# Products with an unread result on TensorE, ahead of q and of each pair's scores, in a block of cached attention

## The chip, the cores and the metric

The kernel runs on one core of a Trainium2 chip. A core has five engines with queues of their own: TensorE (PE; its weight loads are listed as PEld), VectorE (DVE), ScalarE (ACT), GpSimd (POOL) and SyncE (SP), which here only issues transfers. Transfers run on 16 DMA engines. The metric is the time of one execution in device microseconds; the number given for a kernel is the median of its runs.

## The reference

A block of attention with grouped heads over a cache: 8 sequences, 4 new tokens each, 32 query heads, 8 key and value heads, 2048 cached positions, head size 128, everything in bfloat16.

```python
q = (x @ wq).reshape(B, Sq, Hq, Dh).transpose(0, 2, 1, 3)   # x: 8 x 4 x 512, wq: 512 x 4096
k = jnp.repeat(k_cache, 4, axis=1)                          # k_cache, v_cache: 8 x 8 x 2048 x 128
v = jnp.repeat(v_cache, 4, axis=1)
scores = jnp.einsum("bhqd,bhkd->bhqk", q, k) * Dh ** -0.5
o = jnp.einsum("bhqk,bhkd->bhqd", softmax(scores), v)
out = o.transpose(0, 2, 1, 3).reshape(B, Sq, Hq * Dh) @ wo  # wo: 4096 x 512
```

Keys and values are 33.5 MB each, the two weights 4.2 MB each: 75.5 MB are read once.

## The kernel before

The work on the cache goes in eight pairs, one for each sequence `p`, and in sixteen units of values `u`, two for each sequence (four key and value heads each).

**Transfers.** SP issues all loads into one queue, in the order of the program: the keys of pair 0, `x`, `wq`, the keys of pair 1, the values of sequence 0, then for each pair the keys of a later pair (4 MB, `load_pair`, L95) and two units of values (2 MB each, `load_v`, L100), as the buffers come free, and last `wo` in six pieces (`load_wo`, L106, with the list `pieces` at L407). A key buffer is free when VectorE has turned its last tile; a buffer of values when TensorE has used it.

**Start.** TensorE turns `x` by products with an identity (L141, `xtp`), multiplies it with `wq` (`q_products`, L154, 32 products in two groups), and ScalarE, VectorE and GpSimd scale and spread the result over `q_bd` (L168 to L190).

**A pair.** Its keys are turned on VectorE in four tiles `kt` (`turn_keys`, L127; three buffers). Each tile gives eight score products on TensorE (`scores`, L207), 128x512 each, into two PSUM tiles `s_ps`, which ScalarE's exponentials of the pair before must have left. When all four are there, VectorE takes the maxima (L229), ScalarE the exponentials (L248), VectorE turns the probabilities (L262), and ScalarE and GpSimd copy them into a block form (`copy_probs`, L269). The values of a unit are 32 products 128x256 in four quarters (`values`, L312); they run about two pairs behind the scores, as `values_of` (L419) lists. ScalarE divides the result (L332), and `finish` (L342) turns it by one float32 product with 64 columns (`o_t`, L355), which VectorE copies.

**Order.** The order on each engine is that of the program, written by hand. In pair `p`, TensorE has: scores of tiles 0 and 1, two quarters (16 products) of the first unit of values, scores of tile 2, `finish` of the last pair's units, scores of tile 3, then the other quarters of values. In pairs 0, 3 and 4 VectorE turns the next pair's first tile ahead of the maxima (L449).

```python
        scores(p, 0)
        scores(p, 1)
        for quarter in range(2) if vals else ():
            values(vals[0], quarter)
        if (p, 2) not in kts:
            turn_keys(p, 2)
        scores(p, 2)
```

**Tail.** After pair 7, units 11 to 15 of the values run one after the other on TensorE, with `finish` of the unit before within each; then `project` (L396) multiplies with `wo` in the order of its pieces, VectorE and ScalarE copy the result, and SP stores it.

**PSUM.** `xtp`, the two `psq` of q, every `o_t`, and `nat` and `perm` of the tail share two buffers with the tag "m" in the pool `psum_m` (L69): each takes the buffer of the one before the last, and waits until that has been read.

Of the kernel before, what the change touches and what calls it, by code (L numbers as in the profile page):

```python
# [9 lines left out]
FP32 = mybir.dt.float32  # L10
# [4 lines left out]
def kernel(  # L15
# [9 lines left out]
    nc = tc.nc  # L25

    B, Sq, D = x.shape
    _, Hkv, Sk, Dh = k_cache.shape
# [40 lines left out]
    psum_m = ctx.enter_context(tc.tile_pool(name="psum_m", bufs=2, space=bass.MemoryType.PSUM))  # L69
# [8 lines left out]
    ident4 = const.tile([128, 128], FP32, name="ident4")  # L78
# [48 lines left out]
    def turn_keys(p, t):  # L127
        kts[(p, t)] = ktpool.tile([128, CT, 2, 2, SH, 2], BF16, tag="kt", name="kt")
        nc.vector.transpose(  # L129
            kts[(p, t)][:, :, :, :, :, :].rearrange("k c w j s e -> k (c w j s e)").bitcast(FP32),  # L130
            k_sb[p % KB][:, t * CT : (t + 1) * CT, :].rearrange("s c d -> s (c d)").bitcast(FP32),
        )
# [5 lines left out]
    for i in range(XR):  # L138
        row = x_all[:, i * D : (i + 1) * D].rearrange("q (p r) -> q r p", r=R)
        for r in range(R):  # L140
            nc.tensor.matmul(  # L141
                xtp[:, r, i::XR],
                lhsT=row[:, r, :],
                rhs=ident[:T, :T:XR],
                start=True,
                stop=True,
# [4 lines left out]
        v_cache[0].rearrange("(v g) (s c) d -> (g s) v c d", v=VB, c=C),  # L151
    )

    def q_products(j):  # L154
        psq = psum_m.tile([128, rep * Dh], FP32, tag="m", name="psq")
        for r in range(R):
            for g in range(G):
                c0 = (2 * g + j) * rep * Dh
                nc.tensor.matmul(  # L159
                    psq[g * T : (g + 1) * T, :],  # L160
                    lhsT=xT_sb[:, r, :],
                    rhs=wq_sb[:, r, c0 : c0 + rep * Dh],
                    start=(r == 0),
                    stop=(r == R - 1),
                )
        return psq

    def scale_q(psq):  # L168
        q_nat = small.tile([128, rep * 2, 2, S], BF16, tag="q_nat", name="q_nat")
        nc.scalar.mul(  # L170
            out=q_nat[:, :, :, :],
            in_=psq[:, :].rearrange("t (n w e) -> t n e w", w=S, e=2),
            mul=scale,
        )
        return q_nat

    def spread_q(j, q_nat, engines):
        q_t = small.tile([128, rep, 4, B, Sq], BF16, tag="q_t", name="q_t")
        nc.vector.transpose(  # L179
            q_t[:, :, :, :, :].rearrange("w h i b s -> w (h i b s)"),  # L180
            q_nat[:, :, :, :].rearrange("t n e w -> t (n e w)"),
        )
        for g in range(G):
            rows = slice(g * S, (g + 1) * S)
            engines[g](  # L185
                out=q_bd[rows, j, :, :, :, g ^ (2 * j), :].rearrange(
                    "w k e b (h s) -> w (k e b) h s", h=rep
                ),
                in_=q_t[rows, :, :, :, :].rearrange("w h i b s -> w (i b) h s"),
            )  # L190

    by_gpsimd = nc.gpsimd.tensor_copy
    by_three = [by_gpsimd, nc.vector.tensor_copy, nc.scalar.copy] * 3
    q_nats = [scale_q(q_products(j)) for j in range(2)]
    spread_q(0, q_nats[0], by_three)
    spread_q(1, q_nats[1], by_three[1:])
# [10 lines left out]
    def scores(p, t):  # L207
        if t == 0:
            for j in range(2):
                s_pss[(p, j)] = psum_s.tile([128, 2, CT, SH], FP32, tag="s", name="s_ps")  # L210
        for i in range(4):
            k, e = i // 2, i % 2
            for j in range(2):
                h = (t + j) % 2
                nc.tensor.matmul(  # L215
                    s_pss[(p, j)][h * NQ : (h + 1) * NQ, t // 2, :, :],
                    lhsT=q_bd[:, j, k, e, p, :, :].rearrange("k g q -> k (g q)"),
                    rhs=kts[(p, t)][:, :, k, j, :, e],
                    start=(i == 0),
                    stop=(i == 3),  # L220
                )
# [26 lines left out]
    def exponentials(u):  # L248
        s_sbs[u] = small.tile([128, C // 4, S, 2], BF16, tag="s_sb", name="s_sb")
        l_sbs[u] = totals.tile([128, 1], FP32, tag="l_sb", name="l_sb")  # L250
        nc.scalar.activation(  # L251
            out=s_sbs[u][:, :, :, :].rearrange("q a w j -> q a j w"),
            in_=s_pss[u][:, :, :, :].rearrange("q i c s -> q c s i"),
            func=EXP,
            bias=less[u][:, 0:1],
            accum_out=l_sbs[u][:, :],
        )
# [4 lines left out]
    def turn_probs(u):  # L262
        p_ts[u] = turned.tile([128, C // 4, 2, HQ, 2], BF16, tag="p_t", name="p_t")
        nc.vector.transpose(  # L264
            p_ts[u][:, :, :, :, :].rearrange("s x g q j -> s (x g q j)").bitcast(FP32),
            s_sbs[u][:, :, :, :].rearrange("q a s j -> q (a s j)").bitcast(FP32),
        )
# [44 lines left out]
    def values(u, quarter):  # L312
        if quarter == 0:
            o_pss[u] = psum_o.tile([128, 2, Dh], FP32, tag="o", name="o_ps")
        h, a0 = quarter // 2, quarter % 2 * (C // 8)
        for a in range(C // 8):
            c = quarter * C // 4 + 2 * a
            nc.tensor.matmul(  # L318
                o_pss[u][:, :, :].rearrange("n j d -> n (j d)"),
                lhsT=probs_of[u][:, h, a0 + a, :, :, :].rearrange(  # L320
                    "s j g q -> s (j g q)"
                ),
                rhs=vs[u][:, c : c + 2, :].rearrange("s c d -> s (c d)"),
                start=(c == 0),
                stop=(c == C - 2),
            )
# [15 lines left out]
    def finish(u):  # L342
        v, b = units[u]
        o_t = psum_m.tile([128, NQ], FP32, tag="m", name="o_t")
        if u == NU - 1:
            for h in range(2):
                nc.tensor.matmul(
                    o_t[:, :],
                    lhsT=o_scs[u][:, h, :],
                    rhs=ident4[:, h * NQ : (h + 1) * NQ],  # L350
                    start=(h == 0),
                    stop=(h == 1),
                )
        else:
            nc.tensor.matmul(o_t[:, :], lhsT=o_scs[u][:, :], rhs=both[:, :], start=True, stop=True)  # L355
        (nc.scalar.copy if u in (NU - 3, NU - 1) else nc.vector.tensor_copy)(  # L356
            out=oT[v][:, :, :, b, :].rearrange("d (k r) p s -> d p k r s", k=2),
            in_=o_t[:, :].rearrange("d (k p r s) -> d p k r s", k=2, p=2, s=Sq),
        )
# [51 lines left out]
    def all_inverses():  # L411
        while waiting:
            inverses(*waiting.pop(0))

    def softmax_top(u):
        maxima(u)
        exponentials(u)

    values_of = [(), (), (0, 1), (2,)] + [(2 * p - 5, 2 * p - 4) for p in range(4, NPAIR)]  # L419
    after = {w: w + 2 for w in range(NU - 7)}  # L420
    after.update({NU - 6: NU - 4, NU - 5: NU - 3, NU - 4: NU - 2, NU - 3: NU - 1})
# [3 lines left out]
    for p in range(NPAIR):  # L425
        vals = values_of[p]
        for t in range(2):
            if (p, t) not in kts:
                turn_keys(p, t)
        scores(p, 0)  # L430
        scores(p, 1)
        for quarter in range(2) if vals else ():
# [4 lines that stand above are left out]
        turn_keys(p, 3)  # L437
        for w in values_of[p - 1] if p else ():
            finish(w)
        scores(p, 3)  # L440
        if p == NPAIR - 1:
            for u in (NU - 5, NU - 2):
                probs_of[u] = ktpool.tile(
                    [128, 2, C // 4, 2, G, HQ], BF16, tag="kt", name="last_probs"
                )
                words = probs_of[u][:, :, :, :, :, :].rearrange("s x a j g q -> s (x a j g q)")
                nc.gpsimd.memset(words.bitcast(FP32), 0.0)
            copy_probs(NU - 5)
        if p in (0, 3, 4):  # L449
            turn_keys(p + 1, 0)  # L450
        softmax_top((p, 0))
        softmax_top((p, 1))
        for j in range(2):
            turn_probs((p, j))
            if j == 0:
                all_inverses()
        for i, w in enumerate(vals):
            for quarter in range(0 if i else 2, 4):
                values(w, quarter)
            divide(w)  # L460
            if w in after:
                copy_probs(after[w])
            if i == 0:
                waiting += sums(p)
        if p < 2:
            waiting += sums(p)
        if p == 0:
            copy_probs(0)
            copy_probs(1)
        for load in loads_after[p]:  # L470
            (load_pair if load[0] == "p" else load_v)(int(load[1:]))
# [64 lines left out]
```

## Time and profile before

| | |
|---|---|
| time, median of 3 runs | 187.11 us (186.83 to 187.14) |
| profiled execution, its own time | 187.1 us |
| its span, first to last instruction | 185.2 us |
| mean granted TensorE clock over the span | 0.879 |
| TensorE products busy | 124.2 us (67%), 962 instructions |
| TensorE weight loads busy | 80.5 us (43%), 962 instructions |
| VectorE busy | 128.4 us (69%) |
| ScalarE busy | 73.7 us (40%) |
| GpSimd busy | 68.6 us (37%) |
| main DMA queue, share of 16 engines' span | 95.6% |

All times of the profile are from one execution, in us from the start of its span. Busy time of TensorE is modelled from the pipelined products. The clock row gives, for each fortieth of the span, the share of full speed that the throttle granted. A row of a timeline has start, duration, engine, line, operation, written and read tile, shape and count, and in brackets how long the engine was idle before it and which instruction ended that.

### The profile page before, as it was taken

To read this page: it belongs to the slowest core of one execution; us is meant where nothing else is said; L and a number is where in the kernel's file an instruction comes from. 1 tells how busy PE (TensorE), PEld (TensorE's weight loads), DVE (VectorE), ACT (ScalarE), POOL (GpSimd) and SP (SyncE) were. 2 spreads that over 40 slices of the span, in tenths; PEclk is the share of its full clock that TensorE was granted. 3 is DMA by queue.
4 is the path that set the end of the run, shared out by engine and by line. 5 is a ranking of instruction groups with operands and counts; after the bars stand their busy time and mean duration, and the time that the engine had idled before them with its cause. 6 is when DMAs were issued, how large, how long until landed. Compare 5 with 4: busy or idle time off the path is not lost.

```text
span 185.2 us, 2591 instructions
## 1 busy us (share of the span) xinstructions
PE 124.2 (67%) x962; PEld 80.5 (43%) x962; DVE 128.4 (69%) x170; ACT 73.7 (40%) x129; POOL 68.6 (37%) x171
## 2 busy tenths in 40 slices
PE   0002078637505993793499859839985998999993
PEld 0002023212202582362156636715562567988972
DVE  6119335979779788969887798798479857654110
ACT  2000031078060039603900792892089439556030
POOL 8800021028421236322403382470247375872000
PEclk9999999965755899699669999985996599999999
DMA  6999999999999999999989999999999999999950
GB/s 227 453 439 425 432 411 425 428 471 428 403 432 460 446 386 455 412 421 478 446 379 428 442 448 396 432 457 418 435 421 432 432 421 439 428 425 416 420 203 7
DMA packets 4515, 75.71 MB, mean 409 GB/s; under 512 B 500, under 2 KB 660, under 8 KB 916
## 3 DMA queue, kind: packets, MB, share of 16 engines
q1 hardware_dynamic: 4504, 75.57, 95.6%
q8 instruction: 7, 0.11, 0.2%
q14 instruction: 4, 0.03, 0.0%
HBM read 75.53 MB, written 0.03 MB: 408 GB/s over the span
## 4 chain that ended last, share of the span: by engine, by line
PE 49%; DVE 29%; DMA 10%; ACT 5%; issue 5%; SPq 0%; ACTq 0%
PE o_ps L318 28%; DVE kt L129 19%; PE s_ps L215 13%; DMA wq_sb<-in_wq_dram 10%; ACT s_sb L251 4%; DVE top L233 4%; DVE p_t L264 3%; PE out_ps L399 2%; PE psq L159 2%; PE o_t L355 2%; DVE swapped L225 1%; DVE v_both L113 1%; DVE less L239 1%; PE perm L384 1%; PE nat L368 1%
## 5 line engine op out<-in xcount | busy, mean ns | idle before, releaser
L129 DVE STREAM_TRANSPOSE kt<-k_sb 128x2048 f32<-128x2048 f32 x32 | 71.2, 2274 | 10.0 <-DMA k_sb<-in_k_cache_dram 7.9
L215 PE MATMUL s_ps<-kt,q_bd 128*64 128x512 bf16 x256 | 47.3, 492 | 35.6 <-DVE kt L129 23.9
L318 PEld LDWEIGHTS <-probs 128*128 128x128 bf16 x448 | 45.1, 103 | 14.0 <-issue 6.1
L280 POOL COPY probs<-p_t 32x512 bf16<-32x512 bf16 x53 | 32.3, 610 | 43.3 <-PE o_ps L318 41.1
L251 ACT ACTIVATE s_sb<-s_ps,less 128x1024 bf16<-128x1024 f32 x16 | 22.3, 1393 | 64.6 <-DVE less L239 37.3
L215 PEld LDWEIGHTS <-q_bd 128*64 128x64 bf16 x256 | 17.9, 131 | 58.8 <-issue 33.6
L280 ACT COPY probs<-p_t 32x512 bf16<-32x512 bf16 x50 | 30.8, 616 | 1.3 <-DVE p_t L264 0.3
L318 PE MATMUL o_ps<-v_both,probs 128*128 128x256 bf16 x192 | 23.8, 284 | 0.0
L233 DVE TENSOR_REDUCE top<-s_ps 128x1 f32<-128x1024 f32 x16 | 19.4, 1215 | 5.2 <-PE s_ps L215 5.2
L318 PE MATMUL o_ps<-v_more,probs 128*128 128x256 bf16 x160 | 22.1, 302 | 0.0
L225 POOL COPY l_swapped<-l_sb 64x1 f32<-64x1 f32 x32 | 5.8, 180 | 30.5 <-ACT s_sb L251 29.7
L264 DVE STREAM_TRANSPOSE p_t<-s_sb 128x512 f32<-128x512 f32 x16 | 11.3, 709 | 6.8 <-ACT s_sb L251 6.8
L299 POOL TENSOR_TENSOR l_total<-l_sb,l_swapped 32x1 f32<-32x1 f32 x64 | 12.3, 192 | 4.0
L338 ACT ACTIVATE o_sc<-o_ps,r_sb 64x128 f32<-64x128 f32 x28 | 10.1, 359 | 4.7 <-PE o_ps L318 2.8
L356 DVE CAST oT<-o_t 128x64 bf16<-128x64 f32 x14 | 3.1, 225 | 12.0 <-PE o_t L355 12.0
L318 PE MATMUL o_ps<-k_sb,probs 128*128 128x256 bf16 x96 | 11.5, 273 | 0.0
L170 ACT ACTIVATE q_nat<-psq 128x512 bf16<-128x512 f32 x2 | 1.2, 597 | 24.1 <-PE psq L159 24.1
L141 PE MATMUL xtp<-ident,v_both 32*128 32x4 bf16 x32 | 1.2, 169 | 13.8 <-DMA v_both<-in_x_dram 13.8
L159 PE MATMUL psq<-wq_sb,xT_sb 128*32 128x512 bf16 x32 | 3.6, 629 | 8.1 <-DMA wq_sb<-in_wq_dram 8.1
L185 POOL COPY q_bd<-q_t 32x512 bf16<-32x512 bf16 x3 | 2.1, 687 | 18.1 <-DVE q_t L179 18.0
L141 PEld LDWEIGHTS <-v_both 32*128 32x128 bf16 x32 | 1.1, 111 | 13.7 <-issue 13.7
L122 POOL MEMSET probs<- 128x4096 bf16 x2 | 7.0, 3512 | 0.0
(46 smaller groups left out, 85.3 us busy)
## 6 DMA issues: line engine op xcount, KB each, us to landing
k_sb<-in_k_cache_dram SPq DMA_DIRECT2D x8, 4096.0 KB, 19.2
v_more<-in_v_cache_dram SPq DMA_DIRECT2D x6, 2048.0 KB, 22.7
v_both<-in_v_cache_dram SPq DMA_DIRECT2D x4, 2048.0 KB, 21.0
k_sb<-in_v_cache_dram SPq DMA_DIRECT2D x4, 2048.0 KB, 22.1
wq_sb<-in_wq_dram SPq DMA_DIRECT2D x1, 4096.0 KB, 19.3
v_both<-in_v_cache_dram SPq DMA_DIRECT2D x1, 4096.0 KB, 28.0
wo_sb<-in_wo_dram SPq DMA_DIRECT2D x3, 1024.0 KB, 14.9
wo_sb<-in_wo_dram SPq DMA_DIRECT2D x1, 640.0 KB, 16.9
```

The costliest lines, as they stand in the source:

```text
L122: nc.gpsimd.memset(pr[:, :, :, :, :, :], 0.0)
L129: nc.vector.transpose(kts[(p, t)][:, :, :, :, :, :].rearrange("k c w j s e -> k (c w j s e)").bitcast(FP32), k_sb[p % KB][:, t * CT : (t + ...
L159: nc.tensor.matmul(psq[g * T : (g + 1) * T, :], lhsT=xT_sb[:, r, :], rhs=wq_sb[:, r, c0 : c0 + rep * Dh], start=(r == 0), stop=(r == R - 1),)
L215: nc.tensor.matmul(s_pss[(p, j)][h * NQ : (h + 1) * NQ, t // 2, :, :], lhsT=q_bd[:, j, k, e, p, :, :].rearrange("k g q -> k (g q)"), rhs=k ...
L225: engine.tensor_copy(out=out[h * NQ : (h + 1) * NQ, :], in_=in_[(1 - h) * NQ : (2 - h) * NQ, :])
L233: nc.vector.reduce_max(out=top[:, :], in_=s_pss[u][:, :, :, :].rearrange("q i c s -> q (i c s)"), axis=AX,)
L251: nc.scalar.activation(out=s_sbs[u][:, :, :, :].rearrange("q a w j -> q a j w"), in_=s_pss[u][:, :, :, :].rearrange("q i c s -> q c s i"), ...
L264: nc.vector.transpose(p_ts[u][:, :, :, :, :].rearrange("s x g q j -> s (x g q j)").bitcast(FP32), s_sbs[u][:, :, :, :].rearrange("q a s j ...
L280: by[x * G + col](out=probs_of[u][rows, x, :, :, col, :], in_=p_ts[(b, j)][quad * S : (quad + 1) * S, :, col % 2, :, :].rearrange("s x q j ...
L299: nc.gpsimd.tensor_tensor(out=total[rows, :], in0=l_sbs[(p, j)][rows, :], in1=swapped[j][rows, :], op=ADD)
L318: nc.tensor.matmul(o_pss[u][:, :, :].rearrange("n j d -> n (j d)"), lhsT=probs_of[u][:, h, a0 + a, :, :, :].rearrange("s j g q -> s (j g q)"),
L338: nc.scalar.mul(out=to, in_=of, mul=by)
```

## The change

A new function takes one PSUM tile of the pool `psum_m` with the tag "m" and writes `n` products of the float32 identity with itself into it (128x128, each starts and stops its own sum). Nothing reads the tile. It is called with 20 ahead of q's products, and in every pair but the first ahead of the scores of tile 0, with 10, 26, 9, 9, 5, 9 and 9: 97 products in all. They stand in TensorE's order behind the products of the values of the pair before. No other instruction is added, removed or moved on any engine; since the tile takes a turn in the buffers of the tag, some waits of `o_t` and of `psq` name another instruction than before.

```diff
+    def idle_products(n):
+        unread = psum_m.tile([128, 128], FP32, tag="m", name="unread")
+        for _ in range(n):
+            nc.tensor.matmul(
+                unread[:, :], lhsT=ident4[:, :], rhs=ident4[:, :], start=True, stop=True
+            )
+
     def q_products(j):
...
     by_three = [by_gpsimd, nc.vector.tensor_copy, nc.scalar.copy] * 3
+    idle_products(20)
     q_nats = [scale_q(q_products(j)) for j in range(2)]
...
+    idle = [0, 10, 26, 9, 9, 5, 9, 9]
     values_of = [(), (), (0, 1), (2,)] + [(2 * p - 5, 2 * p - 4) for p in range(4, NPAIR)]
...
             if (p, t) not in kts:
                 turn_keys(p, t)
+        if idle[p]:
+            idle_products(idle[p])
         scores(p, 0)
         scores(p, 1)
```

## The prediction

> **What bounds the kernel now.** I read the page first, then the clock by stretches, then TensorE's timeline and the chain of waits around the last two pairs, and last the landings of the loads. Two rows of the page, with the main queue's share:
>
> ```profile
> span 185.2 us, 2591 instructions
> PEclk9999999965755899699669999985996599999999
> DMA  6999999999999999999989999999999999999950
> q1 hardware_dynamic: 4504, 75.57, 95.6%
> ```
>
> The DMA engines are busy from the first slice to the 38th of 40. Still, the last slices are not set by a transfer: TensorE is at 9 there. The clock row has dips in the middle. The windows view puts them at definite places (columns: busy us of PE, PEld, DVE, ACT, POOL, then granted clock, DMA share, GB/s):
>
> ```profile
> 106.40:109.80 3.40, 1.49 (x13) 0.58 (x9) 3.40 (x3) 3.27 (x7) 2.79 (x11) 1.00 1.06 455
> ...
> 123.50:130.20 6.70, 5.56 (x28) 3.05 (x27) 5.48 (x3) 2.40 (x4) 1.03 (x3) 0.50 1.07 462
> 130.30:137.00 6.70, 6.70 (x60) 4.97 (x57) 4.50 (x13) 2.00 (x3) 2.63 (x6) 1.00 0.93 401
> 137.10:140.50 3.40, 1.00 (x10) 0.64 (x7) 2.58 (x2) 3.30 (x8) 1.95 (x11) 1.00 1.00 429
> 140.60:147.30 6.70, 6.15 (x28) 3.03 (x29) 6.70 (x4) 4.01 (x8) 4.00 (x5) 0.50 1.02 435
> ```
>
> The clock is whole or half. It halves after a stretch of 3.4 us in which TensorE was busy for 1.00 us, and it stays whole after one with 1.49 us. It comes back only after a stretch that is nearly full. TensorE's timeline shows what this costs pair 7 (pair 6 has the same half clock from its tile 1 on, 18.4 us earlier):
>
> ```profile
> 140.88 1.92 PE L215 MATMUL s_ps<-kt,q_bd 128*64 128x512 bf16 x8 [2.78 <-DVE kt L129]
> 143.07 1.92 PE L215 MATMUL s_ps<-kt,q_bd 128*64 128x512 bf16 x8 [0.28 <-DVE kt L129]
> 144.92 3.08 PE L318 MATMUL o_ps<-v_both,probs 128*128 128x256 bf16 x16
> 147.93 1.05 PE L215 MATMUL s_ps<-kt,q_bd 128*64 128x512 bf16 x8
> 148.91 0.66 PE L355 MATMUL o_t<-both,o_sc 128*128 128x64 f32 x4
> 149.50 1.05 PE L215 MATMUL s_ps<-kt,q_bd 128*64 128x512 bf16 x8
> ```
>
> Eight score products take 1.92 us at the half clock and 1.05 at the whole one, sixteen value products 3.08 (pair 6: 3.59) against 1.92. The chain shows that this lies on the path:
>
> ```profile
> 138.63 4.40 DVE kt L129 x2
> 143.03 0.04 issue
> 143.07 1.92 PE s_ps L215 x8
> 144.99 3.01 PE o_ps L318 x16
> 148.00 0.99 PE s_ps L215 x8
> 148.98 0.59 PE o_t L355 x4
> 149.57 0.98 PE s_ps L215 x8
> ```
>
> From 156.37 to 182.3 the chain is TensorE alone at the whole clock. What an earlier TensorE would meet there is the last piece of wo (its row among the DMA issues, that piece alone):
>
> ```profile
> L109 SPq DMA_DIRECT2D wo_sb<-in_wo_dram x1: 432/432/432, 163.7 to 163.7; - x1
> ...
> DMA to landing us min/median/max: 15.9/15.9/15.9
> ```
>
> It lands at 163.7 + 15.9 = 179.6. TensorE's last forty projection products run from 179.91 to 182.27, and the last two of them need this piece. So the DMA queue stands 2.4 us behind the path, and that is all the tail can give back.
>
> **The change part by part.** The profiled execution took 187.1 us with a span of 185.2, so 1.9 lie around the span; the median of the three runs is 187.11, the same. I reckon against 187.1.
>
> *The price of a product.* The nearest row is o_t, float32 with 64 columns: four passes take 0.66 us (81.13) and two take 0.43 (97.97), so one more product costs 0.23 at the whole clock. The added one has 128 columns. Lower end 0.23, if the width cost nothing; upper end 0.46, if all of it grew with the width. A pass is a weight load of the same 128x128 and a stream that doubles, so I take 0.34. At the half clock it is twice that. The 97 products are 388 more rows on PE and PEld, 33 us of work at the whole clock, all placed where TensorE waits.
>
> *Twenty ahead of q.* They begin behind xtp, at 14.9, wait for nothing but the identity (made by 2 us), and have until 23.09, when wq lands: 8.1 us. q's 32 products took 3.61 us, about 0.43 for each four of 512 columns, where two score products of that width share 0.24 at the whole clock; so q ran at half although the page's clock row shows 9 there. With 3 to 6 us of it at half the group takes 8.3 to 9.8 us and ends 0.1 to 1.6 us after wq; q then takes 1.8 instead of 3.6: -1.7 to -0.2, and +0.7 with the upper price. All of it at half would be 13.6 us, 5.4 late (the slower rival). I take -1; it decides nothing (next).
>
> *Pairs 1 to 3.* VectorE starts pair 4's first key tile at 82.09. Those keys land just before it: v4, next in the queue, is issued at 67.30 and lands 19.5 later, at 86.8, and 2 MB take 4.9 (landings at 121.0 and 125.9 of two in a row), so the keys land at 81.9. Pair 4's first tile stands ahead of pair 3's maxima on VectorE. So whatever q and pairs 1 to 3 gain beyond 0.2 us is lost here: 0. They lose nothing either: in pair 3 alone (75.74 and 77.59: 1.92 and 2.62 at half) the whole clock takes off 1.6, which covers a late q and 26 products that overrun their 8.09 us before pair 2.
>
> *Pair 4.* The nine products (3.1 us) end near 86, since pair 3's work ends earlier; the scores still wait for ScalarE to free their PSUM tiles at 87.7 and 89.43. That leaves the nearly empty stretch that the trace has there now (0.38 us busy from 85.9 to 89.3, then a half clock). Between 0 and -1.7, which the half-clock rows at 92.37 and 94.22 hold; I take 0.
>
> *Pair 5.* Its five (1.7 us) begin at 104.7 where 0.85 was waited; scores of tile 0 end about 1 us later, but those of tile 1 wait for VectorE until 108.86. 0.
>
> *Pair 6.* Nine products from 119.7 fill 3.1 us of a wait of 2.78. Scores of tile 1 start at 124.65 as before, take 0.98 instead of 1.92, the sixteen value products 1.85 instead of 3.5, tile 2 0.98, the two o_t 0.59, and tile 3 waits for its keys until 128.98 and ends at 130.05 instead of 132.75: -2.7. All of pair 7's VectorE work hangs on that end.
>
> *Pair 7.* By the same sum from 143.07: 144.05, 145.9, 146.9, 147.5, 148.45 instead of 150.55: -2.1. Its keys land at 135.4 (v9 at 116.21 + 24.1, less 4.9), VectorE now comes to them at 138.63, so 2.7 earlier is allowed. Together -4.8 at 156.37.
>
> *The tail.* There v15 (147.4 + 22.3 = 169.7, used at 172.57) allows 2.8 and wo's last piece 2.4. Queues: SP issues its loads behind VectorE's key tiles and TensorE's values, all earlier or unmoved, and a load is always in flight from 0.7 to 179.6, so the 75.6 MB end when they did. After 179.6 come two products, 0.3 us, and the output starts at 179.95 instead of 182.31: -2.35.
>
> *The unread tile* takes a turn in the two buffers of o_t and psq. Its last reader is at least one o_t copy back, done microseconds before; the waits on TensorE's own count that o_t now carries are for products that ended before the scores. 0.
>
> Sum: 187.1 - 2.35 = 184.75.
>
> By the Trainium skill (TensorE: Matmul & The Clock Gate, Part 1 and "Why this matters for your kernels") one idle window of about 3.4 us halves the clock, and gaps under some 3 us keep it whole. The trace disagrees: waits of 2.78 us ahead of pairs 6 and 7 were followed by 0.50. By the skill's rule the filling would gain nothing there, and the sum would be 187.1; I go by the row.
>
> **Rivals.** *Only part of it holds.* The products run in full but the clock falls in pair 6 or 7, because its stretches lie otherwise in another execution. One pair alone gives -2.1 to the cap, but a half clock in part of each gives some -0.5 to -1.6: 185.5 to 186.6. For it: the 1.00 and 1.49 rows are close. Against: with nine products no stretch is under two thirds full.
>
> *Slower: the products don't hold the clock.* They load float32 weights for about a third of their time, and if that counts as idle, the clock halves within the wait and the rest cost 0.68. Half of nine at each price is 4.6 us. Place: ahead of pairs 3, 6 and 7; scores of tile 1 then start 1.5 late and still at half, three times, +4.5: 191.6, and up to 197 with q 5.4 late. It decides when nine products and eight scores outlast 138.1 to 143.03, that is above 0.33 us each with a half clock behind them, 0.44 with a whole one. For it: no row shows float32 work alone. Against: two thirds busy is more than the 1.49 in 3.4 that held.
>
> The Trainium skill (TensorE: Matmul & The Clock Gate, Part 4) says that a transpose by the identity, in its own mode, doesn't bring the whole clock; no run here shows whether a plain float32 product by the identity is like that, and by this rule the time would be this rival's.
>
> *No change.* The waits of 2.78 us are not what halves the clock, so filling them leaves it halved; or the DMA queue stretches by what TensorE gains: 187.1. Against: each half clock follows a nearly empty stretch, VectorE waits for these scores (the chain), and the queue ends 2.4 us early.
>
> **How the numbers follow.** Capped gain, 184.3 to 185.3: 0.62. Part of it, 185.3 to 186.7: 0.21. Within 0.2% (0.37 us, about what can be told from no change): 0.05. Slower: 0.12. Range 184.2 to 186.7, which leaves out the last two; by itself the likeliest case spans 184.3 to 185.3, a DMA end 0.5 either way. Faster 0.83, same 0.05, slower 0.12.
>
> **What would show it.** Right: PEclk whole through pairs 6 and 7, sixteen value products near 1.9 there, the last projection products waiting for wo, which lands near 179.6. Unread passes of 0.11 to 0.23 us apart confirm the price. Wrong: half clock behind the unread products, scores of tile 1 in pair 7 later than VectorE's keys, or wo landing later than 180.

## The result, and the profile after

The changed kernel takes 185.24 us (median of 6 runs, 184.73 to 185.63), the kernel before 187.12 in the same comparison. The ratio is 0.9905, with a 95% interval of 0.988 to 0.9929: faster by 0.7 to 1.2%. (The ratios of this section and the next leave out executions far above the rest of their kernel, and are not quite the quotients of the medians.) The profiled execution took 185.24 us, with a span of 183.3, again 1.9 less than the time.

The rows of the page that answer to those of the kernel before, with the unread products' own groups:

```profile
span 183.3 us, 2984 instructions
PEclk9999999985599699879858996999999999999999
DMA  6999999999999999999999999999999999999980
q1 hardware_dynamic: 4504, 75.57, 96.6%
L157 PE MATMUL unread<-ident 128*128 128x128 f32 x194 | 25.4, 292 | 0.0
L157 PEld LDWEIGHTS unread<-ident 128*128 128x128 f32 x194 | 24.4, 207 | 1.0 <-issue 0.9
```

From the 26th slice on the clock is whole. It still dips in slices 9 to 11, 14, 17 and 18, 20 to 22, and 25. Each of the 97 products is two rows, and the 194 are 25.4 us busy. The windows view (busy us of PE, PEld, DVE, ACT, POOL, then granted clock, DMA share, GB/s) says which pairs this means. Its first two rows are cut where the trace records that the clock changed, at 111.12 and 114.53:

```profile
107.71:111.12 3.41, 1.50 (x13) 0.60 (x10) 3.41 (x3) 3.27 (x7) 2.81 (x11) 1.00 1.06 454
111.12:114.53 3.41, 3.41 (x18) 2.10 (x18) 3.27 (x2) 2.38 (x4) 0.99 (x2) 0.50 0.92 399
114.60:140.50 25.90, 23.79 (x204) 18.18 (x204) 21.01 (x33) 14.39 (x25) 11.66 (x36) 1.00 1.00 428
140.60:147.30 6.70, 5.09 (x42) 2.94 (x42) 6.70 (x4) 4.86 (x10) 4.30 (x6) 1.00 1.00 430
```

Pairs 6 and 7 are whole (last two rows). A half clock that the kernel before did not have stands in pair 5, behind a stretch with 1.50 us of work. TensorE's timeline from pair 5's values on, and in pair 7:

```profile
111.04 3.55 PE L326 MATMUL o_ps<-v_both,probs 128*128 128x256 bf16 x16
...
138.13 2.17 PE L157 MATMUL unread<-ident 128*128 128x128 f32 x18
141.07 1.05 PE L223 MATMUL s_ps<-kt,q_bd 128*64 128x512 bf16 x8 [0.78 <-DVE kt L129]
143.27 1.05 PE L223 MATMUL s_ps<-kt,q_bd 128*64 128x512 bf16 x8 [1.14 <-DVE kt L129]
144.25 1.92 PE L326 MATMUL o_ps<-v_both,probs 128*128 128x256 bf16 x16
146.10 1.06 PE L223 MATMUL s_ps<-kt,q_bd 128*64 128x512 bf16 x8
```

Nine products are over in 2.17 us, 0.24 each, and 0.78 of the wait is left. The scores of tile 1 start 0.2 us later than in the kernel before (143.27 against 143.07) and the scores of tile 2 1.83 earlier (146.10 against 147.93). That is the whole gain of the execution: the start of VectorE's maxima, pair by pair, tells where the time went.

| start of the maxima of pair | 3 | 4 | 5 | 6 | 7 | first product of unit 11 |
|---|---|---|---|---|---|---|
| before | 84.32 | 100.81 | 114.36 | 132.78 | 150.59 | 156.37 |
| changed | 85.37 | 102.00 | 117.19 | 132.98 | 148.77 | 154.55 |
| later (+) or earlier (-) | +1.05 | +1.18 | +2.83 | +0.20 | -1.82 | -1.82 |

So 1.05 are lost up to pair 3, 1.6 in pair 5, and 2.6 and 2.0 gained in pairs 6 and 7. At the end TensorE did not meet wo. The transfer's row for the last piece alone, and TensorE's last products:

```profile
L109 SPq DMA_DIRECT2D wo_sb<-in_wo_dram x1: 432/432/432, 160.9 to 160.9; - x1
...
DMA to landing us min/median/max: 18.6/18.6/18.6
```

```profile
178.09 2.36 PE L407 MATMUL out_ps<-wo_sb,oP 128*32 128x256 bf16 x40
```

The piece lands at 160.9 + 18.6 = 179.5, as before, and TensorE ends at 180.45.

### The profile page after: what moved, and what is told of

It reads as the page before. It is cut to its first block, busy times and chain, and to the rows that moved or that the text cites. A ratio compares the mean times of both kernels' runs of the same rounds, so it can differ in the third digit from the quotient of the medians.

```text
span 183.3 us, 2984 instructions
## 1 busy us (share of the span) xinstructions
PE 139.9 (76%) x1156; PEld 102.6 (56%) x1156; DVE 128.7 (70%) x170; ACT 73.8 (40%) x129; POOL 68.7 (37%) x171
## 4 chain that ended last, share of the span: by engine, by line
PE 45%; DVE 28%; DMA 16%; ACT 4%; issue 4%; SPq 1%; ACTq 0%; DVEq 0%
PE o_ps L326 28%; DVE kt L129 18%; DMA k_sb<-in_k_cache_dram 16%; PE s_ps L223 12%; ACT s_sb L259 4%; DVE top L241 4%; DVE p_t L272 3%; PE out_ps L407 2%; PE o_t L363 2%; DVE swapped L233 1%; DVE v_both L113 1%; DVE less L247 1%; PE perm L392 1%; PE nat L376 1%; SPq L114 0%
## 5 line engine op out<-in xcount | busy, mean ns | idle before, releaser
L223 PE MATMUL s_ps<-kt,q_bd 128*64 128x512 bf16 x256 | 41.0, 437 | 25.0 <-DVE kt L129 14.4
L288 POOL COPY probs<-p_t 32x512 bf16<-32x512 bf16 x53 | 32.4, 612 | 42.5 <-PE o_ps L326 40.4
L223 PEld LDWEIGHTS <-q_bd 128*64 128x64 bf16 x256 | 16.4, 118 | 42.7 <-issue 27.6
L157 PE MATMUL unread<-ident 128*128 128x128 f32 x194 | 25.4, 292 | 0.0
L157 PEld LDWEIGHTS unread<-ident 128*128 128x128 f32 x194 | 24.4, 207 | 1.0 <-issue 0.9
L326 PE MATMUL o_ps<-v_both,probs 128*128 128x256 bf16 x192 | 24.5, 288 | 0.0
L326 PE MATMUL o_ps<-v_more,probs 128*128 128x256 bf16 x160 | 20.7, 290 | 0.0
## 6 DMA issues: line engine op xcount, KB each, us to landing
wo_sb<-in_wo_dram SPq DMA_DIRECT2D x1, 640.0 KB, 18.6
```

What stands on the lines that cost most here:

```text
L157: nc.tensor.matmul(unread[:, :], lhsT=ident4[:, :], rhs=ident4[:, :], start=True, stop=True)
L223: nc.tensor.matmul(s_pss[(p, j)][h * NQ : (h + 1) * NQ, t // 2, :, :], lhsT=q_bd[:, j, k, e, p, :, :].rearrange("k g q -> k (g q)"), rhs=k ...
L288: by[x * G + col](out=probs_of[u][rows, x, :, :, col, :], in_=p_ts[(b, j)][quad * S : (quad + 1) * S, :, col % 2, :, :].rearrange("s x q j ...
L326: nc.tensor.matmul(o_pss[u][:, :, :].rearrange("n j d -> n (j d)"), lhsT=probs_of[u][:, h, a0 + a, :, :, :].rearrange("s j g q -> s (j g q)"),
```

## The experiments

The theory after the result: the groups ahead of pairs 6 and 7 make the gain by holding the clock, wo's last piece is the floor, and what pair 5 and the start lose has causes of its own. The rivals: the changed turns of the PSUM buffers make the gain; the early groups carry it; the early groups cause the losses; the half clocks are hidden.

**One product in each group.**

```diff
-    idle_products(20)
+    idle_products(1)
-    idle = [0, 10, 26, 9, 9, 5, 9, 9]
+    idle = [0, 1, 1, 1, 1, 1, 1, 1]
```

> Every group cut to one product: the unread tile takes its turns in the shared PSUM buffers and the waits stand as in the changed kernel, but only 0.24 us of each wait is filled. Clock theory (the groups gain only by keeping the clock whole): the half clocks of the kernel before come back in pairs 6 and 7, 187.1 us, 186.8 to 187.5. Rival (the gain comes from the buffers' turns or from the changed waits): 185.2 as the changed kernel.

Measured: 186.52 us (185.03 to 188.28), ratio 0.9969, interval 0.9931 to 1.0007, which includes no change. In the profile both pairs have their half clock back (pair 7's tile 1 takes 1.92 us again). The buffers and the waits alone don't give the gain. The median lies 0.3 below the expected range, and three runs near 185.05 lie under everything seen of the kernel before: a single product may already keep the clock in some executions. That was not followed up.

**Pairs 6 and 7 alone, and all but them.**

```diff
-    idle_products(20)
-    idle = [0, 10, 26, 9, 9, 5, 9, 9]
+    idle = [0, 0, 0, 0, 0, 0, 9, 9]
```

> Only the nine products ahead of pairs 6 and 7 are kept. Clock theory: start and pair 5 as before, -2.7 in pair 6 and -2.1 in pair 7, and the end is held by wo's last piece: 184.8 us, 184.3 to 185.2, so no slower than the changed kernel. Rival (the earlier groups carry part of the gain, since a whole clock up to pair 5 brings pair 6 forward): 185.8 to 186.5.

Measured: 184.63 us (184.54 to 185.08), ratio 0.989, interval 0.9858 to 0.9923. Eighteen products give all that the 97 give. The profile is that of the slowest run: pair 6 is whole, but pair 7 still has a half clock in tile 1 (1.89 us) and the values (2.72). Nine products leave 0.77 us of the wait ahead of tile 0 empty, and 1.13 are waited ahead of tile 1. Here both lie in one stretch of the clock, which holds 1.50 us of work (this kernel's rows, cut at the clock's changes):

```profile
138.09:141.50 3.41, 1.50 (x14) 0.72 (x14) 3.41 (x3) 3.27 (x8) 2.92 (x7) 1.00 0.99 423
141.50:144.92 3.42, 3.42 (x16) 1.75 (x16) 3.42 (x2) 1.22 (x2) 1.48 (x1) 0.50 1.02 436
```

```diff
-    idle = [0, 10, 26, 9, 9, 5, 9, 9]
+    idle = [0, 10, 26, 9, 9, 5, 0, 0]
```

> The groups ahead of q and of pairs 1 to 5 are kept, those ahead of pairs 6 and 7 are left out. If the early groups gain nothing and cost nothing: 187.1 us. If they cost what the profile of the changed kernel shows (pair 4's first key tile 1.06 us later, pair 5's values at half the clock, 1.6 us), and pairs 6 and 7 run at half as before: 188.1 to 189.9. If they carry the gain: under 186.5.

Measured: 187.11 us (186.58 to 189.57), ratio 1.0012, interval 0.9975 to 1.0049. The 79 products ahead of q and of pairs 1 to 5 gain nothing that can be measured, and on the whole cost nothing either. Together the two runs settle the place: pairs 6 and 7.

**Pair 7 alone.**

```diff
-    idle_products(20)
-    idle = [0, 10, 26, 9, 9, 5, 9, 9]
+    idle = [0, 0, 0, 0, 0, 0, 0, 9]
```

> Only the nine products ahead of pair 7. By the sum of the prediction -2.1 from the kernel before; by the profiles since, where nine products last 2.17 us and the clock fell in pair 7 behind them in two of three kernels, only -0.8 to -2.1: 185.0 to 186.3. Pair 6 at half clock as before. Rival (pair 7's half clock is hidden): 187.

Measured: 185.74 us, ratio 0.9908, interval 0.9863 to 0.9954; seven of ten runs took 184.87 to 185.97, three 188.41 to 188.67. The profile has the half clock in pair 6 (tile 1 1.92 us, sixteen values 3.60) and none in pair 7 (1.05 and 1.92). Pair 7's share is on the path. The scatter stays; that pair 6, which is left as it was, makes it is not shown.

**Pair 5 filled.**

```diff
         scores(p, 0)
+        if p == 5:
+            idle_products(8)
         scores(p, 1)
```

> The changed kernel with eight more products (1.9 us at the whole clock) in pair 5, between the scores of tile 0 and of tile 1, where its profile has 1.91 us of wait and then a half clock. If that half clock cost it 1.6 us of the path: pair 5's sixteen value products take 1.92 instead of 3.55 us, and the time falls until wo's last piece holds the end: 184.4 us, 184.0 to 184.8. Rival (pair 5's half clock is hidden, or its place is chance from run to run): 185.2 as the changed kernel.

Measured: 185.94 us (185.63 to 186.25), ratio 0.995, interval 0.9924 to 0.9975. The half clock in pair 5 was gone (sixteen values 1.92 instead of 3.55 us), and yet this median lies above the changed kernel's. The trace shows a late transfer: of the 16 parts in which wo's last piece lands, 15 were there by 179.4, the last at 180.79. TensorE's last forty products, begun at 178.54, took 2.58 us. And a 16 KB piece of TensorE's own instructions was fetched at 177.24, in 0.97 us. All profiles have such fetches, one for about 256 of TensorE's instructions: 7 in the kernel before, 9 in the changed one, which has 388 more. In this execution the late part alone accounts for little: pair 7 had a half clock (its sixteen values took 2.92 us), and without the late part forty products from 178.54 at 2.36 us would have ended only 0.2 us sooner. But none of the twelve runs took less than 185.63. The next three runs test whether that fetch held wo back.

**The same kernel with fewer instructions ahead of the end.**

```diff
-    idle = [0, 10, 26, 9, 9, 5, 9, 9]
+    idle = [0, 10, 6, 9, 9, 5, 9, 9]
         scores(p, 0)
+        if p == 5:
+            idle_products(8)
         scores(p, 1)
```

> The kernel that fills pair 5 (185.94 us), with 6 products ahead of pair 2 instead of 26, so 80 instructions fewer ahead of the end: the last fetch of TensorE's program moves from 177.2 to about 179.2, behind wo's pieces. Theory: wo's last piece lands near 179.5 again and the time is 184.7 us, 184.4 to 185.1. Rival (eight products in pair 5 cost time themselves): 185.9.

Measured: 184.75 us, ratio 0.9892, interval 0.9852 to 0.9932. The ninth fetch stood at 179.15, wo's last piece landed at 179.54. As expected; the eight products themselves cost nothing.

**As many instructions, but in pair 2.**

```diff
-    idle = [0, 10, 26, 9, 9, 5, 9, 9]
+    idle = [0, 10, 34, 9, 9, 5, 9, 9]
```

> The changed kernel with 34 products ahead of pair 2 instead of 26, and nothing in pair 5: as many instructions as the kernel that filled pair 5 and took 185.94 us, so the ninth fetch of TensorE's program falls at about 177.2 again. If that fetch was what cost that kernel, wo's last piece lands near 180.8 and the time is 185.9 us, 185.6 to 186.3. If the eight products in pair 5 were it: 184.7 to 185.3.

Measured: 185.99 us (185.61 to 186.36), ratio 0.9954, interval 0.992 to 0.9988. The ninth fetch stood at 175.79 and wo's last piece landed at 180.74. TensorE, which needed the pieces at 177.7, waited (timeline of this kernel):

```profile
177.06 0.61 PE L407 MATMUL out_ps<-wo_sb,oP 128*32 128x256 bf16 x8
178.32 1.05 PE L407 MATMUL out_ps<-wo_sb,oP 128*32 128x256 bf16 x16 [0.64 <-DMA wo_sb<-in_wo_dram]
179.84 1.23 PE L407 MATMUL out_ps<-wo_sb,oP 128*32 128x256 bf16 x16 [0.47 <-DMA wo_sb<-in_wo_dram]
```

Eight products more in a wait of pair 2, some 120 us ahead of the end, cost 0.7 to 1.2 us there (against 185.24 and, below, 184.75 of the changed kernel, the latter on another chip; the kernel before took 186.7 on this one and 186.8 on that): by the length of the program, not by the work.

**A fetch at the same moment in the short kernel.**

```diff
-    idle_products(20)
-    idle = [0, 10, 26, 9, 9, 5, 9, 9]
+    idle = [0, 0, 20, 0, 0, 0, 9, 9]
```

> Twenty products ahead of pair 2 are added to the kernel that has only the nine ahead of pairs 6 and 7 (184.63 us). They lie in a wait of 8 us, and pair 4's first tile covers an overrun. Their 80 instructions move the last 16 KB piece of TensorE's program, which one DMA engine fetched at 179.25, to about 177, among the last pieces of wo. Theory (such a fetch holds back that engine's share of the loads by about 1 us): wo's last piece lands near 180.7 instead of 179.5 and the time is 185.7 us, 185.3 to 186.2. Rival (the late wo of the kernel that fills pair 5 had another cause): 184.6.

Measured: 184.7 us, ratio 0.9895, interval 0.9862 to 0.9928. This expectation failed. The fetch came as meant, at 177.41, but it was the eighth, and wo's last piece landed at 179.48. So a fetch among wo's pieces doesn't always hold them back. The 16 parts of a load don't end together: in the kernel before the last piece's parts land from 177.58 to 179.58, so a fetch through a part that is early would be hidden. Whether the eighth goes by such an engine is not in the trace; it stays open.

**The changed kernel once more.** No edit.

> The changed kernel itself, on the chip of these runs: 185.2 us, 184.7 to 185.7. If what pair 5 loses depends on where the clock's stretches fall, its profile may show the half clock in pair 4, 5 or 7; the fetches of TensorE's program stand at the same instructions as in its first profile, so the keys of pair 1 land near 33.7 again.

Measured: 184.75 us (184.53 to 185.61), ratio 0.9919, interval 0.9889 to 0.9948. This profile has the same program and no half clock behind pair 4's (the middle two rows are cut on the clock's grid):

```profile
89.10:95.80 6.70, 5.05 (x22) 2.36 (x22) 6.15 (x4) 3.59 (x8) 1.82 (x10) 0.50 0.94 403
106.10:109.51 3.41, 1.50 (x15) 0.86 (x12) 3.41 (x3) 3.26 (x8) 2.75 (x12) 1.00 1.01 435
109.51:112.93 3.42, 3.42 (x30) 2.10 (x27) 3.42 (x2) 2.78 (x5) 2.39 (x5) 1.00 0.95 412
...
140.60:147.30 6.70, 6.70 (x58) 4.33 (x55) 5.91 (x6) 3.58 (x6) 4.60 (x4) 1.00 1.00 430
```

```profile
108.86 1.05 PE L223 MATMUL s_ps<-kt,q_bd 128*64 128x512 bf16 x8 [1.91 <-DVE kt L129]
109.84 1.92 PE L326 MATMUL o_ps<-v_both,probs 128*128 128x256 bf16 x16
```

The same wait of 1.91 us in pair 5 that halved the clock in the first profile left it whole here, and the sixteen values took 1.92 instead of 3.55. The clock's changes in the trace lie on a grid of 3.41 us, and the grid stands 1.6 us apart in the two executions, counted from the start of the span. The stretch around the wait holds 1.50 us of work in both, and also in the kernel before, whose clock held:

```profile
106.38:109.79 3.41, 1.50 (x13) 0.60 (x9) 3.41 (x3) 3.28 (x7) 2.79 (x11) 1.00 1.06 454
109.79:113.20 3.41, 3.41 (x30) 2.36 (x28) 3.41 (x3) 2.50 (x5) 2.31 (x4) 1.00 1.02 442
```

What differs is the place of the wait: it begins 0.43 us after the start of its stretch in the first profile, 0.85 in this one and 0.57 in the kernel before. In all, ten profiles of the study have this wait whole within one stretch. In seven it began 0.56 us or more after the start and the clock held; in three it began 0.43 or less after it and the clock fell. So pair 5's loss is no property of the program; it goes with where the grid falls in an execution. Here TensorE caught up with wo: its last piece lands at 179.63, and the chain breaks the projection in two where the third-last piece lands (178.65).

```profile
177.27 1.42 PE out_ps L407 x24
178.69 0.01 issue
178.70 1.29 PE out_ps L407 x16
179.99 0.02 issue
180.01 0.41 DVE out_sb L515
```

**The waits of pairs 6 and 7 filled, and work added in the tail.**

```diff
-    idle_products(20)
-    idle = [0, 10, 26, 9, 9, 5, 9, 9]
+    idle = [0, 0, 0, 0, 0, 0, 12, 12]
         scores(p, 0)
+        if p >= 6:
+            idle_products(4)
         scores(p, 1)
```

> Pairs 6 and 7 alone, their waits filled: twelve products (2.9 us) ahead of tile 0 and four (1.0 us) between tiles 0 and 1. No half clock from pair 6 on, and the end held by wo's last piece at 179.5: 184.6 us, and all runs within 184.4 to 185.0, where nine products left runs up to 185.1. Rival (the products cost time once the waits are full): 185.2 or more.

Measured: 184.76 us (184.59 to 185.21), ratio 0.9888, interval 0.9837 to 0.9939. The clock is whole from 95.6 on, and the chain ends with wo itself:

```profile
156.95 21.66 DMA wo_sb<-in_wo_dram
178.62 0.04 issue
178.66 1.26 PE out_ps L406 x16
```

No better than nine products: the end does not depend on TensorE any more. The next kernel adds to this one:

```diff
     for w in range(NU - 5, NU):
+        if w == NU - 4:
+            idle_products(6)
```

> The kernel with the waits of pairs 6 and 7 filled, with six products (1.45 us at the whole clock) more in the tail, between units 11 and 12 of the values, where TensorE waits for nothing that the profile of the kernel before shows. If wo's last piece holds the end, with TensorE some 2 us ahead of it, they cost 0 to 0.4 us: 184.6 to 185.0. If TensorE's chain holds it, they cost 1.45: 186.1.

Measured: 184.79 us, ratio 0.991, interval 0.9875 to 0.9945. Six more products (1.50 us in the profile), in the middle of a stretch in which TensorE never waited in the kernel before, cost nothing in the median. The profile of the kernel without these six shows the room: TensorE waits 0.82 us ahead of 160.08 and again for the load of the last values, which lands at 169.73:

```profile
169.77 1.91 PE L325 MATMUL o_ps<-k_sb,probs 128*128 128x256 bf16 x16 [0.81 <-DMA k_sb<-in_v_cache_dram]
```

Seven of ten runs took 184.55 to 185.13, three 185.98 to 186.09. The profile is of one of these three, and it has the half clock in pair 5 (sixteen values 3.49 us), though this kernel has no product ahead of pair 6. With that loss TensorE waits nowhere in the tail, and the work there does count. So the floor is the transfers, the last values before wo. With the clock held, TensorE waits 1.6 us in all on the way to it, and pair 5's half clock can use that up.

**The kernel before once more.** No edit.

> The kernel before itself, for a second profile. If the clock is granted by stretches of 3.41 us whose place is free of the program, the half clocks stand at other places of pairs 4 to 7 than in its first profile, and the time is anywhere from 185.8 to 188.5. If their place follows the program alone, they stand in pairs 4, 6 and 7 again: 187.1.

Measured: 186.37 us (185.45 to 188.24), ratio 0.9963 to the other runs of the kernel before, interval 0.9919 to 1.0007. Its profile again has the half clock in pairs 6 and 7:

```profile
123.20:129.80 6.60, 5.55 (x26) 2.87 (x23) 5.57 (x3) 2.47 (x5) 1.08 (x2) 0.50 1.02 442
140.20:146.90 6.70, 6.03 (x27) 2.98 (x28) 6.70 (x4) 4.00 (x8) 4.12 (x5) 0.50 1.01 428
```

This did not tell the two expectations apart by place: the grid happened to lie only 0.4 us from that of the first profile. The times do speak for chance, since the kernel before scatters from 185.5 to 188.6 over the study, and the two kernels with products in pairs 6 and 7 alone (nine each, and twelve with four) from 184.54 to 185.21.

## Why the prediction was right or wrong

*Direction and size.* Forecast 184.75, measured 185.24 at first and 184.75 in the second set; that the second meets the forecast to the hundredth is luck, since the prediction itself left the end of the transfers open by 0.5 us either way. The mechanism was right: the half clock in pairs 6 and 7 was on the path, filling the waits removes it (pairs 6 and 7 alone: 0.989), and it was worth 2.6 and 2.0 us where 2.7 and 2.1 were forecast. The -4.8 forecast at the first product of unit 11 came in full only where pair 5 lost nothing: -1.82 in the first profile, -4.66 in the second (151.71).

*The floor.* Right: wo's last piece landed at 179.4 to 179.6 in all profiles but two, and with the clock held the chain ends in wo. The other limit that the prediction named, the load of the last values (v15), binds ahead of it: in the second profile TensorE waits 0.72 us for it and starts on these values at 169.86 instead of 172.57. The first profile, whose time is the median, did not get there; it ended 0.5 us later than the forecast because of the next three points.

*Pair 5, "0".* Wrong for the first profile: +1.6. The prediction looked only at the scores that wait for VectorE, not at the wait of 1.91 us between tiles 0 and 1 as a stretch that can halve the clock; the kernel before has the same wait, with the same 1.50 us of work in its stretch, and its clock held. The second profile, the same program, has 0. In part this is the rival "only part of it holds", put at 0.21, whose cause was named (stretches that lie otherwise) but not its place, pair 5.

*Pairs 1 to 3, "they lose nothing".* Wrong by 1.05 us in the first profile and 0.25 in the second (maxima of pair 3 at 84.57). The cover was to be pair 3 at the whole clock, but in the first profile pairs 2 and 3 still ran at half from their tiles 1 on. The groups end too early (26 products: 6.07 us of a wait that had been 8.09), because of the price. And the keys of pair 1 landed at 33.73 instead of 32.71, which the sum did not have at all: VectorE waited 2.66 us for them.

*The price of a product, 0.34.* Mis-sized: 0.24 at the whole clock (2.17 us for nine), and 0.22 for one more by the way that the prediction reckoned (18 rows take 2.17 us, ten 1.28), just under its lower end of 0.23. Doubling the columns of the stream cost nothing. Ahead of q, 40 rows took 6.82 us instead of the 8.3 to 9.8 reckoned, so q started on time and took 1.91 us.

*The products that might not hold the clock.* This rival fell. The clock became whole at 18.96 with nothing but these products running from 14.6 on, and stayed whole behind the groups of pairs 6 and 7 in both profiles of the changed kernel.

*"With nine products no stretch is under two thirds full."* Wrong, by the price: at 0.24 nine products leave 0.77 of a wait of 2.8 empty, and a stretch that takes in this rest and the 1.13 ahead of tile 1 holds 1.5 us of work, 44%. Of the eight profiles with nine products ahead of pair 7, four have a half clock in pair 7 (pairs 6 and 7 alone, pair 5 filled, and the two kernels that follow it with other numbers in pair 2). So the half clock that the rival "only part of it holds" named did come in these executions. The time shows little of it: in the two of these kernels whose wo landed on time the medians are 184.63 and 184.75. TensorE waits 1.6 us for other work in the tail where the clock holds, which can take up such a loss.

*No change.* Fell with the ratio of pairs 6 and 7 alone.

*The skill's rule.* The Trainium skill (TensorE: Matmul & The Clock Gate, Part 1) has a window of about 3.4 us with a phase that is free of the kernel. The trace agrees: stretches of 3.41 us, and a grid at another place in the second profile of the same program. Its short form (section "Why this matters for your kernels"), that gaps under some 3 us keep the clock, does not hold here: waits of 2.78 us lost it, and even 1.91 us did in one of two executions. How busy TensorE is over the whole stretch is what the rows follow, though not to the last. Cut on each trace's own grid, from its first recorded change of the clock on, the 14 profiles have 58 stretches at the whole clock with up to 1.34 us of work, and all were followed by a half clock; none with 1.58 or more was. Of the 23 from 1.48 to 1.57, 14 were and nine were not. So the 1.00 and 1.49 of the prediction are no two sides of a sharp limit, and what decides in between stays open.

## What to carry to other kernels

Read the clock by stretches, cut where the trace itself changes the clock: a window that is 0.1 us off (107.80 to 111.10 in the first profile of the changed kernel) shows 1.39 us of work where the stretch holds 1.50, and suggests a limit where there is none. Count how much work a stretch holds rather than how long one wait is, and leave a margin. Then find out which half clocks lie on the path, since 18 of these 97 products did all the work. Filling is free only where the engine waits, and only up to the next floor: look up when the last transfer lands before counting a gain in full. Filler also lengthens the program, and the program is itself fetched by transfers, which can hold back those of the data.

## What the runs showed of the hardware that was not expected

- *The program's own loading can delay the data's.* Every 256 or so instructions of TensorE a 16 KB piece is fetched by DMA, in 0.9 to 1.0 us as a rule. Ahead of the landing of pair 1's keys the first fetch fell at 26.7 to 27.1 in the kernels with the 20 products ahead of q, and the keys landed at 33.4 to 33.8; where it fell at 32.4 to 32.9, at the very end of that load, they landed at 32.4 to 32.7. In one kernel, with the fetch at 32.03, they landed at 34.03. One of the 16 parts was late each time, the others were not. At the end of the kernel a ninth fetch at 175.8 or 177.2 put wo's last piece off from 179.5 to 180.8, and the time by about 1 us; an eighth at 175.4 to 177.8 (four profiles) did not, for a reason that stays open.
- *Scatter.* One kernel with no change at all took from 185.5 to 188.6 us. That the place of the clock's stretches sets most of this is argued from the two profiles of the changed kernel, not shown for the kernel before.
- *Float32 products.* One more of 128x128 by 128 columns takes 0.22 us at the whole clock, against 0.23 for one more with 64 columns. In the group ahead of q the rows start 0.21 us apart until the clock becomes whole at 18.96, and 0.11 from then on.
